# Attention with spatial reduction, then a gated feed-forward: query groups 8 to 11 turned by DMA, and the chunks lent to VectorE placed anew

## The chip, the cores and the metric

The kernel runs on one core of one Trainium2 chip. The metric is the device time of one execution in microseconds (us). Three runs of the kernel before gave a median of 942.97 us (942.91 to 943.38). One more execution was recorded by the hardware profiler. The engines are called PE (TensorE), DVE (VectorE), ACT (ScalarE), POOL (GpSimd) and SP (SyncE, which here only issues DMAs).

## The reference, cut to what matters

```python
# q (4, 12288, 128); kv (4, 384, 32, 128); w_sr (128, 128); w_in (128, 2048); w_out (2048, 128), all float32
kv_pool = kv.reshape(B, H // 4, 4, W // 4, 4, C).mean(axis=(2, 4))   # 4x4 mean: 768 keys per batch
k = v = kv_pool.reshape(B, -1, C) @ w_sr
s = (q @ k.transpose(0, 2, 1)) / sqrt(C)
a = softmax(s)                                                       # over the 768 keys
x = (a @ v).reshape(B * 12288, C)                                    # 49152 rows of 128
h = x @ w_in
out = (h * sigmoid(1.702 * h)) @ w_out
```

So each query row is compared with 768 pooled keys of its batch, the weighted values become a row of x, and each row of x goes through a feed-forward layer with 2048 hidden values.

## The kernel before, in words

The 49152 rows are cut into 96 groups of 512 rows (`NG`, `G`), and four groups make a slice (`SG`, 24 slices, `NS`). The attention of a group has 6 chunks (`JC`) of 128 keys; its feed-forward part has 16 chunks (`FCH`) of 128 hidden values. A chunk is one tile of 128 x 512. It is *filled* by one matmul of 512 columns into PSUM (L402 for attention, L688 for the feed-forward part), and one ACT instruction, over one, two or three chunks, applies the exponential (L404) or the gated activation (L690) and writes bfloat16 into a frame of `ag`. Later it is *drained*: four matmuls of 129 columns per attention chunk against values and a column of ones (L416), one matmul of 512 columns per feed-forward chunk against `w_out` (L698). `ag` has room for 102 chunks, so the drains can lag far behind the fills.

The work goes in two rounds (`R`): attention of groups 0 to 47, their feed-forward part, then the same for groups 48 to 95. Within the first round the six chunks of groups 0 to 7 are not in order of groups, since the keys come in chunk by chunk; they are listed by hand at L743, all 48 ahead of group 8. The first two ACT instructions take one chunk, the next 77 two, the others three (L742).

Not all chunks go through ACT. Those in the list `rolling` (attention) and `lent` (feed-forward) are computed on DVE from a PSUM bank by a chain of elementwise operations, 8 per exponential (`early_exp`) and 15 per gated activation (`lent_gelu`), and kept in the small tile `aside` instead of `ag`. Groups 48 to 51 (`early`) are computed on DVE wholly. A group whose last chunk is lent can only be drained to its end when the chain on DVE is done.

All instruction streams are written out by one planner, the loop at L885, which keeps a clock of its own with fixed costs (`COST`, `COPY`, `FIXED`, `CHUNK`), fills two steps ahead, and puts drains, transposes, pooling and DVE chains between the fills. The order on each engine is therefore fixed when the program is built; on the chip an engine runs its own stream in order and waits where a semaphore is not yet set. The tables `first`, `TURN`, `SUM`, `CAST` and `CAST_MOE` say by hand at which fill or at which group something is issued. A `gate()` (L593) is a one-element memset on DVE followed by one on POOL that waits for it: it holds back what POOL issues next until DVE has come to that place of its stream.

The fill of a group needs its queries with the 128 features on the partitions, in the tile `qT` of its slice (four buffers). There are two ways to get there:

- `load_q` (L265, POOL's queue, casting on the way) puts rows of float32 `q` as bfloat16 into a part of the tile `x`; `transpose_q` (L272) then turns a group with four PE transposes into PSUM and one copy into `qT` (by DVE; by ACT for group 0). Groups 0 to 9 come so.
- `cast_q` (L246, POOL's queue) writes a slice of `q` as bfloat16 into the DRAM tensor `q_bf`; `load_qT` (L251) turns the slice by one DMA transpose on SP's queue into `qT`, behind a memset of one column by DVE. Slices 3 and up come so. Groups 10 and 11, the second half of slice 2, come by `cast_q(2, 2)` and `load_rest(2, 2)` (L257), issued when group 5 begins.

POOL's queue at the start holds, in this order: queries of groups 0 to 7 mixed with chunks 1 to 5 of the keys and values (1 MB of float32 each), the load of groups 8 and 9, the cast of the second half of slice 2, the casts of slices 3 and 4, and behind a gate the cast of slice 5. SP's queue holds the first chunk of the keys, `w_sr`, then the DMA transposes in the order of the slices. The PE transposes of groups 8 and 9 are handed to the planner at fills 23 and 25 (`later`).

Of the kernel before, what the change touches and what calls it, by code (L numbers as in the profile page):

```python
# [26 lines left out]
def kernel(  # L27
# [8 lines left out]
    JC = J // 128  # L36
    d_ff = moe_w_in.shape[1]
    FCH = d_ff // 128
# [77 lines left out]
    def x_tile(s):  # L116
        return x[:, s % XS * SG:(s % XS + 1) * SG]
# [20 lines left out]
    def load_chunk(b, jc):  # L138

        a, ch = divmod(jc, HC)  # L140
        if b and jc in wide:
            nc.gpsimd.dma_start(out=wide[jc], in_=kv_r[b, a, ch])
            return
        t = x_tile(spots[jc] if b else XS - 1 - jc)
        nc.gpsimd.dma_start(out=t, in_=kv_r[b, a, ch])
        kv_tiles[b, jc] = t.rearrange("p (wp w1 c) -> p w1 wp c", w1=r, c=C)
# [12 lines left out]
    def add_row(jc):  # L159

        last, wp = False, None
        t = wide[jc].rearrange("p (wp e) -> p wp e", wp=r)
        narrow_sum = wide[jc].bitcast(BF).rearrange("p (wp e) -> p wp e", wp=r)[:, :, 4 * C:5 * C]
        for m in (0, 2):
            nc.vector.tensor_tensor(t[:, m:m + 2, 0:2 * C], t[:, m:m + 2, 0:2 * C], t[:, m:m + 2, 2 * C:4 * C], ADD)
            yield 3.2
        nc.vector.tensor_tensor(narrow_sum, t[:, :, 0:C], t[:, :, C:2 * C], ADD)
        added[jc] = narrow_sum
        extras.extend([(pool_added, 1, jc), (key_and_value, 1, jc)])
        last = True  # L170
        yield 3.3
# [34 lines left out]
    def add_kv(b, n):  # L206
        i, w = divmod(n, r)
        if n == 0:
            kv_sums[b] = kvs[0:Hp]
        for i2 in range(2):  # L210
            nc.gpsimd.dma_start(out=kv_sums[b][:, i2], in_=kv_p[b, i, w, :, i2],  # L211
                                **({"accum_op": ADD} if n else {}))
# [33 lines left out]
    def cast_q(s, lo=0):  # L246
        sl = slice(s * SG + lo * G, (s + 1) * SG)
        nc.gpsimd.dma_start(out=q_bf[sl, :].rearrange("(p i) c -> p (i c)", p=128),
                            in_=q_flat[sl, :].rearrange("(p i) c -> p (i c)", p=128))

    def load_qT(s):  # L251
        qTs[s] = qpool.tile([128, 1, SG], BF, name="qT")
        nc.vector.memset(qTs[s][:, 0, 0:1], 0.0)
        nc.sync.dma_start_transpose(out=qTs[s], in_=q_bf[s * SG:(s + 1) * SG, :])


    def load_rest(s, lo):  # L257
        qTs[s] = qpool.tile([128, 1, SG], BF, name="qT")
        nc.vector.memset(qTs[s][:, 0, lo * G:lo * G + 1], 0.0)
        nc.sync.dma_start_transpose(out=qTs[s][:, :, lo * G:], in_=q_bf[s * SG + lo * G:(s + 1) * SG, :])  # L260

    QS = 3
    qs = [x_tile(XS - 1 - JC - s) for s in range(QS)]

    def load_q(s, lo, hi):  # L265
        nc.gpsimd.dma_start(  # L266
            out=qs[s].rearrange("p (g e) -> p g e", g=4)[:, lo:hi, :],
            in_=q_flat[s * SG + lo * G:s * SG + hi * G, :].rearrange("(g p i) c -> p g (i c)", p=128, i=4))
# [30 lines left out]
    load_chunk(0, 3)  # L299
    load_chunk(0, 4)  # L300
    load_chunk(0, 5)
    load_q(2, 0, 2)
    cast_q(2, 2)
    cast_q(3)
    cast_q(4)

    ones = cpool.tile([128, 32], BF)
    nc.vector.memset(ones, 1.0)
# [70 lines left out]
        return K * len(free_frames())  # L379

    early = range(NG // R, NG // R + EARLY)
    rolling = [(i, JC - 1) for i in (28, 44, 45, 58, 59, 71, 73, 75, 95)]
    lent = [(g, FCH - 1) for g in (3, 7, 11, 13, 17, 19, 52, 53, 55, 56, 58, 60, 62, 65, 67, 69, 71, 72, 75, 77, 79, 81, 83, 84, 86, 88, 91, 93)]
    turn = [("a",) + c for c in rolling if c[0] < early[0]] + [("m",) + c for c in lent if c[0] < early[0]]
    turn += [("a",) + c for c in rolling if c[0] > early[-1]] + [("m",) + c for c in lent if c[0] > early[-1]]
    aside = agpool.tile([128, K, 512], BF, name="aside")
# [96 lines left out]
    def new_raw():  # L483
        nonlocal raw
        raw = qpool.tile([128, 1, SG], BF, name="qT")[:, 0, 0:2 * G].bitcast(F32)
# [75 lines left out]
    def early_fits(p, i, jc):  # L561
        if (i, jc) in rolling:
            group = seq[p][1][0][0] if seq[p][0] == "a" else seq[p][1][0][0] // (NG // R) * (NG // R) + NG // R - 1
            return (i // GB, jc) in vs and (i in turned or i // 4 in qTs and (i // 4 - 1 <= group // 4 if i >= 4 * QS else i - 2 <= group)) and len(used) > turn.index(("a", i, jc)) - K
        if (i, jc) in lent:
# [9 lines left out]
    def put_away(n, m):  # L575
        size = PART // 2 if n == 0 and m > FIRST + 1 else PART
        for o in range(m * PART, m * PART + PART, size):
            lo = n * XS * SG + o * T
            nc.sync.dma_start(out=x_bf[lo:lo + size * T, :].rearrange("(k p) c -> p k c", p=T),
                              in_=x[:, o * T:(o + size) * T].rearrange("p (k c) -> p k c", k=size))  # L580

    def bring_back(n, m):
        o = m * PART
        lo = n * XS * SG + o * T
        nc.sync.dma_start_transpose(out=x[:, o * T:(o + PART) * T].unsqueeze(1), in_=x_bf[lo:lo + PART * T, :])
# [7 lines left out]
    def gate():  # L593

        one = gate_tile[:, gates[0] % 8:gates[0] % 8 + 1]
        gates[0] += 1
        nc.vector.memset(one, 0.0)  # L597
        nc.gpsimd.memset(one, 0.0)  # L598

    TURN = {8: 3, 9: 4, 10: 5, 20: 6, 21: 7, 22: 8, 25: 9, 32: 10, 35: 11, 42: 12}  # L600
    SUM = {14: (0,), 15: (1,), 16: (2,), 17: (3,), 20: (4,), 21: (5,)}
    CAST = {0: [5], 13: [6], 14: [7], 15: [8], 16: [9], 26: [10, 11], 27: [12]}
    CAST_MOE = {20: 13, 21: 14, 22: 15, 23: 16, 33: 17, 34: 18, 35: 19, 36: 20, 37: 21, 38: 22, 39: 23}

    def background(i):

        first_round = i < GB * 2
        s = TURN.get(i, NS) if first_round else i // 4 + 3 if i % 4 == 0 else NS
        if s < NS:
            load_qT(s)  # L610
        if i == 5:
            load_rest(2, 2)
        if i in CAST:
            gate()
            for s in CAST[i]:
                cast_q(s)
        if i in (10, 12):
            gate()
            for jc in range(i % 10 * 3 // 2, i % 10 * 3 // 2 + 3):
                load_chunk(1, jc)  # L620
        for jc in SUM.get(i, ()):
            if jc in wide:
                sums.append(add_row(jc))
            else:
                extras.extend([(pool_chunk, 1, jc), (key_and_value, 1, jc)])
        if i in (28, 33, 38):
            put_away(0, (i - 28) // 5)
        if i in (31, 36, 41):
            bring_back(0, (i - 31) // 5)
        if i == 40:  # L630
            new_raw()
        if 4 * XS - LEAD <= i < 4 * XS:
            gate()
            add_kv(2, i - 4 * XS + LEAD)
        if i == 28:
            gate()
            nc.gpsimd.dma_start(out=w_in_sb, in_=moe_w_in)
        if i == 29:
            gate()
            nc.gpsimd.dma_start(out=w_out_sb, in_=moe_w_out.rearrange("(o p) c -> p o c", p=128))  # L640

    def background_moe(g):
# [16 lines left out]
        if g == 43:  # L659
            raw = None  # L660
            background(early[0])
# [19 lines left out]
    extras = []  # L681
# [102 lines left out]

    begun = set()

    def later(g):
        extras.append((transpose_q, g))

    def jobs(p):  # L790

# [9 lines left out]
    def prepare(p):  # L801
# [24 lines left out]
        16: [(key_and_value, 0, 4)],  # L826
        17: [(pool_chunk, 0, 5)],
        20: [(key_and_value, 0, 5)],
        23: [(later, 8)],
        25: [(later, 9)]}  # L830

# [51 lines left out]
    for n in range(len(seq)):  # L885
        fill(n + 2)
        jobs(n + 3)
        while True:
# [34 lines left out]
            kind, i, c = source[0]  # L923
# [58 lines left out]
```

## Time and profile before

| | |
|---|---|
| median of 3 runs | 942.97 us (942.91 to 943.38) |
| the profiled execution | 943.09 us |
| its span | 941.3 us |
| matmuls and PE transposes | 6218 |
| matmuls of 512 columns, L688 and L402 on ACT's side | 1508 and 543 |
| PE transposes of queries, L280 | 40 (ten groups) |
| activations, L690 and L404 | 506 and 208 |
| chunks on DVE from the lists: `lent`, `rolling` | 28, 9 |
| DMA transposes of queries, L254 and L260 | 21 and 1 |
| mean granted PE clock | 1.00 |

The span is what the profiler recorded from the first to the last instruction; the execution's own time is 1.8 us longer. In rows of the timeline the first number is the start in us from the span's start, the second the length; behind engine, line and operation stand the tiles written and read, and x how many instructions were merged. A matmul's length includes its way through the pipeline, so the distance between starts tells more than the length. In rows on DMAs the last number is the median time from issue to landing in us. POOL's and SP's issue rows (POOL L248, SPq L254) are the issue alone; the transfer goes on behind them.

### The profile page before, as it was taken

Reading aid. Unit: us, or ns where it says so; the run is one execution under the profiler, and the core shown is the slowest. Engines: PE = TensorE matmul, PEld = TensorE weight load, DVE = VectorE, ACT = ScalarE, POOL = GpSimd, SP = SyncE. Lnnn points to the kernel's source line nnn. Section 1 sums busy time; section 2 is a strip of 40 time slices with the busy share of each in tenths; the row PEclk is TensorE's granted clock in tenths of the full one; section 3 lists DMA queues with packets and bytes.
Section 4 is the critical chain, followed back from the end, with each engine's and each line's share of the span. In section 5 each row is a group of like instructions: output and inputs, shape, how many; then the busy total and the mean of one; then the engine's idle time right before and its main releaser. Section 6 shows DMA issues by size and latency. Waiting matters only on the chain.

```text
span 941.3 us, 15464 instructions
## 1 busy us (share of the span) xinstructions
PE 935.8 (99%) x6218; PEld 499.4 (53%) x6218; DVE 616.4 (65%) x1236; ACT 928.9 (99%) x722; POOL 75.2 (8%) x127
## 2 busy tenths in 40 slices
PE   9999999999999999999999999999999999999998
PEld 5777775444444444454447777744444444444444
DVE  6776376437477777777235755478787778778761
ACT  6999999999999999999999999999999999999998
POOL 3401014200003320000000000000000000000000
PEclk9999999999999999999999999999999999999999
DMA  9998969937679992774324956371222222222122
GB/s 211 223 285 180 197 140 136 136 73 157 145 145 173 165 129 39 120 124 94 62 57 104 172 130 135 70 133 34 42 38 35 44 34 45 34 40 41 33 46 45
DMA packets 379463, 99.91 MB, mean 106 GB/s; under 512 B 353536, under 2 KB 376960, under 8 KB 378272
## 3 DMA queue, kind: packets, MB, share of 16 engines
q1 hardware_dynamic: 350784, 64.06, 36.0%
q0 software_dynamic: 28336, 34.74, 22.1%
q8 instruction: 48, 0.79, 0.3%
q14 instruction: 23, 0.19, 0.1%
q10 hardware_dynamic: 272, 0.13, 0.0%
HBM read 52.49 MB, written 49.81 MB: 109 GB/s over the span
## 4 chain that ended last, share of the span: by engine, by line
PE 92%; ACT 6%; DMA 1%; POOL 0%; issue 0%; DVE 0%; POOLq 0%
PE banks L698 35%; PE banks L688 35%; PE banks L416 11%; PE banks L402 10%; ACT ag L404 6%; DMA x<-in_kv_dram 1%; PE banks L479 1%; PE banks L473 1%; PE banks L726 0%; PE banks L280 0%; PE banks L154 0%; POOL x L266 0%; PE banks L339 0%; PE banks L239 0%; DVE o_sb L734 0%
## 5 line engine op out<-in xcount | busy, mean ns | idle before, releaser
L690 ACT ACTIVATE ag<-banks 128x1536 bf16<-128x1536 f32 (+1 forms) x506 | 676.0, 1497 | 0.0
L688 PE MATMUL banks<-x,w_both 128*128 128x512 bf16 x1508 | 408.0, 379 | 0.0
L698 PE MATMUL banks<-ag,w_both 128*128 128x512 bf16 x1492 | 405.9, 379 | 0.0
L404 ACT ACTIVATE ag<-banks 128x1536 bf16<-128x1536 f32 (+2 forms) x208 | 246.0, 1365 | 3.4 <-PE banks L402 3.2
L698 PEld LDWEIGHTS <-w_both 128*128 128x128 bf16 x1520 | 148.6, 98 | 178.7 <-issue 1.1
L688 PEld LDWEIGHTS <-w_both 128*128 128x128 bf16 x1508 | 146.6, 98 | 172.2 <-issue 0.4
L416 PEld LDWEIGHTS <-ag 128*128 128x128 bf16 x2268 | 147.4, 98 | 49.6
L416 PE MATMUL banks<-v,ag 128*128 128x129 bf16 x2268 | 166.8, 220 | 0.0
L709 DVE STREAM_TRANSPOSE o_sb<-banks 128x512 f32<-128x512 f32 x95 | 67.9, 715 | 134.8 <-PE banks L698 132.6
L402 PE MATMUL banks<-qT,kT 128*128 128x512 bf16 x543 | 151.0, 379 | 0.3 <-DVE kT L187 0.2
L444 DVE RECIPROCAL rec<-banks 128x3 f32<-128x3 f32 x118 | 21.1, 179 | 83.5 <-PE banks L416 83.4
L447 DVE TENSOR_TENSOR x<-banks,rec 128x384 bf16<-128x384 f32 x118 | 65.8, 558 | 4.1
L402 PEld LDWEIGHTS <-kT 128*128 128x128 bf16 x543 | 45.2, 98 | 19.1 <-issue 0.7
L211 POOL DMA_DIRECT2D kvs<-in_kv_dram x32 | 40.3, 1278 | 54.8 <-DMA kvs<-in_kv_dram 54.2
L513 DVE SCALAR_TENSOR_TENSOR eb<-ea 128x512 f32<-128x512 f32 x61 | 42.1, 690 | 2.0
L509 DVE SCALAR_TENSOR_TENSOR eb<-ea 128x512 f32<-128x512 f32 x61 | 42.1, 690 | 1.8
L511 DVE SCALAR_TENSOR_TENSOR ee<-eb,ee 128x512 f32<-128x512 f32 x61 | 42.0, 688 | 1.7
L711 POOL DMA_DIRECT2D out_dram<-o_sb x2 | 1.3, 672 | 514.0 <-DVE o_sb L709 514.0
L519 DVE TENSOR_SCALAR ea<-banks 128x512 f32<-128x512 f32 x33 | 22.8, 692 | 27.0 <-PE banks L479 26.7
L530 DVE TENSOR_SCALAR qT<-banks 128x512 f32<-128x512 f32 x28 | 19.4, 692 | 30.1 <-PE banks L473 29.5
L598 POOL MEMSET gate_tile<- 1x1 f32 x38 | 8.8, 231 | 263.2 <-DVE gate_tile L597 263.2
L502 DVE TENSOR_SCALAR ea<-ea 128x512 int32<-128x512 f32 x61 | 26.7, 438 | 2.0
(96 smaller groups left out, 415.8 us busy)
## 6 DMA issues: line engine op xcount, KB each, us to landing
out_dram<-o_sb SPq DMA_DIRECT2D x378, 64.0 KB, 1.9
kvs<-in_kv_dram POOLq DMA_DIRECT2D x32, 384.0 KB, 6.5
q_bf<-in_q_dram POOLq DMA_DIRECT2D x21, 512.0 KB, 8.1
x_bf<-x SPq DMA_DIRECT2D x13, 768.0 KB, 5.6
x<-in_kv_dram POOLq DMA_DIRECT2D x6, 512.0 KB, 13.9
x<-in_kv_dram POOLq DMA_DIRECT2D x3, 1024.0 KB, 10.7
x_bf<-x SPq DMA_DIRECT2D x6, 384.0 KB, 4.7
x<-in_kv_dram SPq DMA_DIRECT2D x1, 1024.0 KB, 5.1
```

The lines of the kernel that those rows point to most:

```text
L211: nc.gpsimd.dma_start(out=kv_sums[b][:, i2], in_=kv_p[b, i, w, :, i2], **({"accum_op": ADD} if n else {}))
L402: nc.tensor.matmul(ps[:, k, :], kTs[i // GB][:, jc * 128:(jc + 1) * 128], rhs, start=True, stop=True)
L404: nc.scalar.activation(place([("a",) + c for c in chunks]), ps, AF.Exp, scale=scale)
L416: nc.tensor.matmul(av_of[u][:, k * (C + 1):(k + 1) * (C + 1)], weights(("a", i, jc))[:, o:o + T], vs[i // GB][:, jc, 0:C + 1], start=(jc = ...
L447: (nc.gpsimd if split else nc.vector).tensor_tensor(to, ps[:, :, 0:C], rec.unsqueeze(2).broadcast_to([128, TS, C]), MUL)
L509: nc.vector.scalar_tensor_tensor(b, a, P2[0], a, ADD, MUL)
L511: nc.vector.scalar_tensor_tensor(e, b, P2[1], e, ADD, MUL)
L513: nc.vector.scalar_tensor_tensor(b, a, P2[2], a, ADD, MUL)
L688: nc.tensor.matmul(ps[:, k, :], w_in_sb[:, fc * 128:(fc + 1) * 128], x[:, g % (4 * XS) * G:(g % (4 * XS) + 1) * G], start=True, stop=True)
L690: nc.scalar.activation(place([("m",) + c for c in chunks]), ps, AF.Gelu_apprx_sigmoid)
L698: nc.tensor.matmul(o_of[g], w_out_sb[:, fc, :], weights(("m", g, fc)), start=(fc == 0), stop=(fc == FCH - 1))
L709: nc.vector.transpose(o_sb, o_of.pop(g))
```

## The change

Groups 8 and 9 no longer come through `x` and PE. The whole slice 2 is cast to `q_bf` by one `cast_q(2)`, in the place of POOL's queue where the load of groups 8 and 9 and the half cast stood, and `load_qT(2)` is issued when group 0 begins, as the third instruction of SP's queue, where it waits for that cast. The casts of slices 3, 4 and 5 leave the start of POOL's queue: each is issued behind a gate of its own, handed to the planner at fills 18, 21 and 24. One of three places in `x` that held queries is no longer used so (`QS`). The lists change: `rolling` has 12 chunks instead of 9, `lent` 26 instead of 28, mostly at other groups.

```diff
-    QS = 3
+    QS = 2
     qs = [x_tile(XS - 1 - JC - s) for s in range(QS)]
...
     load_chunk(0, 5)
-    load_q(2, 0, 2)
-    cast_q(2, 2)
-    cast_q(3)
-    cast_q(4)
+    cast_q(2)
...
-    rolling = [(i, JC - 1) for i in (28, 44, 45, 58, 59, 71, 73, 75, 95)]
-    lent = [(g, FCH - 1) for g in (3, 7, 11, 13, 17, 19, 52, 53, 55, 56, 58, 60, 62, 65, 67, 69, 71, 72, 75, 77, 79, 81, 83, 84, 86, 88, 91, 93)]
+    rolling = [(i, JC - 1) for i in (32, 40, 47, 56, 57, 67, 68, 71, 78, 86, 89, 91)]
+    lent = [(g, FCH - 1) for g in (3, 6, 7, 11, 13, 17, 53, 54, 57, 59, 60, 65, 67, 69, 71, 72, 75, 77, 79, 81, 83, 85, 86, 89, 91, 93)]
...
-    CAST = {0: [5], 13: [6], 14: [7], 15: [8], 16: [9], 26: [10, 11], 27: [12]}
+    CAST = {13: [6], 14: [7], 15: [8], 16: [9], 26: [10, 11], 27: [12]}
...
-        if i == 5:
-            load_rest(2, 2)
+        if i == 0:
+            load_qT(2)
...
-    def later(g):
-        extras.append((transpose_q, g))
+    def cast_later(s):
+        gate()
+        cast_q(s)
...
         20: [(key_and_value, 0, 5)],
-        23: [(later, 8)],
-        25: [(later, 9)]}
+        18: [(cast_later, 3)],
+        21: [(cast_later, 4)],
+
+        24: [(cast_later, 5)]}
```

The lines from L306 to L786 stand 3 lines earlier in the changed kernel: L402 is L399 there, L416 is L413, L698 is L695.

## The prediction

> **What bounds the kernel now.** I read the page's head first, then the chain, then who waited for whom on ACT and PE.
>
> ```profile
> span 941.3 us, 15464 instructions
> PE 935.8 (99%) x6218; PEld 499.4 (53%) x6218; DVE 616.4 (65%) x1236; ACT 928.9 (99%) x722; POOL 75.2 (8%) x127
> PE 92%; ACT 6%; DMA 1%; POOL 0%; issue 0%; DVE 0%; POOLq 0%
> ```
> ```profile
> ACT x L329 <- DMA x<-in_kv_dram: 3.8, 1, 3.8
> ACT ag L404 <- PE banks L402: 3.2, 3, 2.3
> ```
>
> PE and ACT are both busy for 99%, and all of ACT's larger waits lie before 13.5 us. A busy PE could hide gaps, so I looked at starts in the timeline (start, length, engine, line, operands, count).
>
> ```profile
> 914.83 0.81 PE L688 MATMUL banks<-x,w_both 128*128 128x512 bf16 x3
> 915.48 0.81 PE L698 MATMUL banks<-ag,w_both 128*128 128x512 bf16 x3
> 916.13 0.81 PE L688 MATMUL banks<-x,w_both 128*128 128x512 bf16 x3
> ```
>
> Three matmuls start every 0.65 us, 0.216 each, without a hole. Counting the built program's PE stream with 0.216 per 512-wide matmul and 0.057 per 129-wide one gives some 922 us behind 12.8 us, where the trace needs 925: PE loses about 3 us to everything behind the start. So a shorter program must be shorter on PE and on ACT, and any wait of PE is added in full. DVE (65%) does not bound.
>
> **The start, where the change sits.** All 48 chunks of groups 0 to 7 go first, in 2 activations of one chunk and 23 of two; group 8's first pair is the next.
>
> ```profile
> 25.73 35.08 ACT L404 ACTIVATE ag<-banks 128x1024 bf16<-128x1024 f32 x38
> 30.93 0.39 PE L280 MATMUL banks<-ident,x 128*128 128x128 bf16 x4
> 31.16 0.39 PE L416 MATMUL banks<-v,ag 128*128 128x129 bf16 x4
> 32.83 0.39 PE L280 MATMUL banks<-ident,x 128*128 128x128 bf16 x4
> 33.05 0.39 PE L416 MATMUL banks<-v,ag 128*128 128x129 bf16 x4
> 33.28 0.59 PE L402 MATMUL banks<-qT,kT 128*128 128x512 bf16 x2
> ```
>
> The pair at 33.28 is group 8's: counting pairs in the PE stream gives its place, and ACT, at 0.92 per pair, takes it near 33.9. The two L280 rows are the transposes of groups 8 and 9. In the changed kernel this pair needs the whole DMA transpose of slice 2 (groups 8 to 11); its place in the stream stays, within 0.01 us of PE work.
>
> **The change, part by part.**
> (a) Eight PE transposes go: 31.16 - 30.93 and 33.05 - 32.83, 0.23 and 0.22, together -0.45 us on a saturated PE. Their two DVE copies (0.69 each, hidden) go too.
> (b) Chunks: 3 more exponentials and 2 fewer gelus run on DVE, so ACT has one chunk less: the built program has one 512-wide activation fewer, and as many 1536- and 1024-wide ones in sum.
>
> ```profile
> L690 ACT ACTIVATE ag<-banks 128x1536 bf16<-128x1536 f32 (+1 forms) x506 | 676.0, 1497 | 0.0
> ```
> 676.0/506 is 1.34 per three chunks; less the 0.92 of a pair, a chunk is 0.42, with its fixed part about 0.49. ACT so shrinks as PE does, and the sum takes -0.46 for (a) and (b) together. Bounds: 0 if PE's tail takes it back, -0.5. DVE loses 2 chains of 15 and gains 3 of 8 operations, at most 0.7 each: less work on an engine with 35% free. The placing itself costs nothing while chains end before their drains; if one is late, PE waits. The trace has no such wait, so its price is bounded by one operation's 0.7 below and a chain's remaining 8 x 0.7 = 5.6 above; I take 0.
> (c) The load of groups 8 and 9 (256 KB in bfloat16) and the half cast of slice 2 become one cast of slice 2 in the same place of POOL's queue. Here are their issues in that order, and what the landing view answers for these issues:
>
> ```profile
> 10.00 0.70 POOL L266 DMA_DIRECT2D x<-in_q_dram  x1 [1.92 <-DMA x<-in_kv_dram]
> 11.27 0.51 POOL L248 DMA_DIRECT2D q_bf<-in_q_dram  x1 [0.57 <-DMA x<-in_q_dram]
> 16.29 0.49 POOL L248 DMA_DIRECT2D q_bf<-in_q_dram  x1 [0.69 <-DMA x<-in_q_dram]
> ```
> ```profile
> q_bf<-in_q_dram POOLq DMA_DIRECT2D x1, 256.0 KB, 15.3
> ...
> q_bf<-in_q_dram POOLq DMA_DIRECT2D x1, 512.0 KB, 17.8
> ```
> The half cast lands at 11.27 + 15.3 = 26.6, the last of the three casts behind it at 34.1. As the new cast reads what both old transfers read, I take its landing at 26.5 (26.0 to 27.0).
> (d) SP then issues the transpose of 2048 rows. What this costs alone, and what beside casts, three rows show: the old half transpose, slice 3, and slice 6.
>
> ```profile
> 26.66 1.24 SPq L260 DMA_TRANSPOSE qT<-q_bf  x1
> 34.46 1.83 SPq L254 DMA_TRANSPOSE qT<-q_bf  x1
> 67.49 2.85 SPq L254 DMA_TRANSPOSE qT<-q_bf  x1
> 56.16 0.49 POOL L248 DMA_DIRECT2D q_bf<-in_q_dram  x1
> ```
> ```profile
> qT<-q_bf SPq DMA_TRANSPOSE x1, 8.4
> qT<-q_bf SPq DMA_TRANSPOSE x1, 4.2
> qT<-q_bf SPq DMA_TRANSPOSE x1, 5.4
> q_bf<-in_q_dram POOLq DMA_DIRECT2D x1, 512.0 KB, 14.1
> ```
> Alone: 34.46 + 4.2. Half the rows beside three casts: 8.4, landing at 35.1, that is 1.0 behind the last cast (34.1). Slice 6 beside the end of a cast: 67.49 + 5.4 = 72.9, 2.6 behind that cast (56.16 + 14.1 = 70.3). So a transpose that shares the engines with casts has landed 1.0 to 2.6 behind the last of them.
> (e) Casts 3, 4 and 5 were queued by 16.3 us; now each waits for a small DVE memset. By the new DVE stream these stand behind chunk 5's copy, behind one and behind five of the L428 sums that follow its keys and values:
>
> ```profile
> 26.01 0.29 DVE L157 CAST pTc<-banks 128x128 bf16<-128x128 f32 x1 [0.24 <-PE banks L154]
> 28.69 0.28 DVE L202 CAST v<-banks 128x128 bf16<-128x128 f32 x1
> 28.89 2.26 DVE L428 TENSOR_TENSOR ag<-banks,ag 128x387 f32<-128x387 f32 x4
> 419.26 0.09 POOL L598 MEMSET gate_tile<- 1x1 f32 x1 [7.38 <-DVE gate_tile L597]
> 419.49 0.49 POOL L248 DMA_DIRECT2D q_bf<-in_q_dram  x1
> ```
> ```profile
> q_bf<-in_q_dram POOLq DMA_DIRECT2D x1, 512.0 KB, 5.2
> ```
> From gate to cast is 0.3, so they are issued near 26.6, 29.8 and 32.0, and a cast with no queue ahead lands 5.2 later: 31.8, 35.0, 37.2. On POOL nothing behind them is due before 35.2 (the first L447). Slices 3 to 5 are turned from 34.5 on and needed from 45 on: hidden by 6 us. The buffers and SP's waits of those later turns are the same as before.
>
> The cast of slice 3 thus starts within 0.2 us of the transpose of slice 2, and the next two follow at 3.2 and 2.2 us. Alone the transpose lands at 26.5 + 4.2 = 30.7, 2.6 before 33.28; that margin is what one cast costs. Beside cast 3 alone it would land at 31.8 + (1.0 to 2.6) = 32.8 to 34.4; beside casts 3 and 4 at 36.0 to 37.6; beside all three at 38.2 to 39.8. The old half transpose was held up by all that was queued when it was issued. Cast 4 starts while the new, twice as long one is still held by cast 3, so I take two casts, at the near end, 36.0: a wait of 36.0 - 33.3 = 2.7 us, before which PE cannot start and behind which all its drains stand.
>
> **Weighing a rule.** The rows show a transpose behind casts. The Trainium skill, "DMA: Bandwidth & Descriptors", section on queues, rings and completion order, says that each DMA engine takes turns between its queues by whole packets. The rows on packets bear on it (queue, packets, MB, share of 16 engines; a window with one cast, and one with one transpose):
>
> ```profile
> q0 software_dynamic: 32, 0.52, 44.6%
> ...
> q1 hardware_dynamic: 2080, 0.52, 81.7%
> ```
> A cast is 2 packets per engine, in a 6.6 us window 2.9 us of each engine; the transpose is 130 small ones, 2.6 us. If turns are taken, each cast that arrives before the transpose ends puts its whole 2.9 us in front: 27.8 + 2.6 + 3 x 2.9 = 39.1, all three casts, a wait of 5.8. By that rule the time is the second rival's. The slow 8.4 us transpose agrees with it, the 5.4 us one only in part.
>
> **The sum.** The profiled execution took 943.09, its span 941.3 and 1.8 around it; the median is 0.12 less. 943.09 - 0.46 + 2.7 = 945.3, against the median 945.2. I call a change under 0.2% (1.9 us, 941.1 to 944.9) no difference that can be told.
>
> **Rivals.**
> 1. Not slower: the casts share instead of blocking, and the transpose, held by cast 3 at most, lands at 30.7 to 34.4. The wait is 0 to 1.1, the time 942.97 - 0.46 + (0 to 1.1) = 942.5 to 943.6. For it: the 5.4 us row, only 1.2 over the one alone. Against: the 8.4 us row with half the rows. It decides if the landing is before 35.7. Chance 0.30.
> 2. All three casts in front: landing 38.2 to 39.8, wait 4.9 to 6.5, time 947.4 to 949.0. For it: the old transpose did end behind all of them. Against: cast 5 is issued only at 32.0. Chance 0.15.
> 3. The new places leave a DVE chain late, and PE waits up to 5.6: 942.5 to 948.1, most likely near 945. Against: DVE has less to do, and the trace shows no such wait now. Chance 0.07.
> 4. Faster by over 0.2%: the 3 us that PE loses behind the start come back through the new places, 942.97 - 0.46 - (1.5 to 3) = 939.5 to 941.0. For it only the count above. Chance 0.08.
>
> **How the numbers follow.** My forecast, casts 3 and 4 in front, has 0.40: 944.9 to 946.7. Slower by over 0.2% is that (0.40), rival 2 (0.15) and most of rival 3 (0.05): 0.60. Within 0.2%: 0.30 and the rest of rival 3, 0.32. Faster: 0.08. The range leaves out rival 4 and the far end of rival 2: 942.3 to 948.0.
>
> **What would show it.** Right: PE at group 8's first pair (L399 there) waits some 2.7 us for the transpose of slice 2, ACT shows one wait of about 2 us near 34, and the landing of that transpose takes 9 to 10 us. Cast 3 is issued near 26.6. Wrong: a landing before 33.3 and no wait; a new DVE wait in PE's list; or ACT idle elsewhere. From the wait on, both streams should run as before, shifted, with the last activations 0.5 us earlier against it.

## The result, and the profile after

The changed kernel takes 945.84 us (median of 7 runs, 945.45 to 947.18), the kernel before, run beside it, 943.11 us (7 runs, 942.91 to 943.38). The ratio is 1.0033, with a 95% interval of 1.0021 to 1.0044: slower by 2.7 us by the medians, where 2.2 had been predicted. Two of the seven runs, at 947.1 and 947.2 us, showed a granted clock of 0.998 against 0.999 to 1.000 in the others. The profiled execution took 946.05 us.

The head of the page after and its chain line:

```profile
span 944.3 us, 15325 instructions
PE 929.6 (98%) x6096; PEld 499.2 (53%) x6210; DVE 609.1 (65%) x1228; ACT 928.7 (98%) x721; POOL 74.5 (8%) x128
...
PE 54%; ACT 42%; DMA 3%; issue 1%; DVE 0%; POOL 0%; POOLq 0%
```

The span grew from 941.3 to 944.3. The weight loads (6210 for 6218) and the activations (721 for 722) show that the work did shrink; PE's own busy time can't be compared, since about a hundred of its records are missing here. The chain's DMA share went from 1% to 3%; why its ACT share went from 6% to 42% is left open. Who waited for whom on PE, and on ACT:

```profile
PE banks L399 <- DMA qT<-q_bf: 2.9, 1, 2.9
...
PE banks L476 <- DMA qT<-q_bf: 0.3, 1, 0.3
```
```profile
ACT ag L401 <- PE banks L399: 3.8, 3, 2.9
```

These two rows of PE are new; no other wait of PE's list has changed by more than 0.2 us. In the timeline (start, length, engine, line, operands, count, and the idle time before with what ended it):

```profile
26.44 0.51 POOL L248 DMA_DIRECT2D q_bf<-in_q_dram  x1
26.70 4.88 SPq L254 DMA_TRANSPOSE qT<-q_bf  x1
36.22 0.60 PE L399 MATMUL banks<-qT,kT 128*128 128x512 bf16 x2 [2.93 <-DMA qT<-q_bf]
113.60 0.39 PE L476 MATMUL banks<-qT,kT 128*128 128x512 bf16 x1 [0.29 <-DMA qT<-q_bf]
```

Group 8's first pair waits 2.93 us for the transpose of slice 2. At 113.6 the chunk of group 40, one of the new places in `rolling`, waits 0.29 for slice 10's. The landing view for the window in which cast 3 (the cast of slice 3) and that first transpose are issued (KB and us from issue to landing):

```profile
q_bf<-in_q_dram POOLq DMA_DIRECT2D x1, 512.0 KB, 5.2
qT<-q_bf SPq DMA_TRANSPOSE x1, 9.5
```

26.7 + 9.5 = 36.2. What held it up is in the packets that started in windows of 0.4 us (queue, packets, MB, share of 16 engines, by the whole length of the packets that start there): the windows from 32.4, 32.8 and 35.2 us.

```profile
q1 hardware_dynamic: 452, 0.12, 127.1%
...
q0 software_dynamic: 16, 0.52, 607.8%
q1 hardware_dynamic: 80, 0.02, 22.5%
...
q0 software_dynamic: 32, 0.52, 613.2%
q1 hardware_dynamic: 32, 0.00, 7.8%
```

The transpose has 2080 packets. By the trace's records 2048 of them have 256 bytes, which are its whole 0.52 MB, and 32 have 4 bytes. None moved before 30.4, while cast 3's 16 large ones, started from 27.6 to 28.8, were under way. From 30.4 to 33.2 all but 32 of them went. At 32.8 each of the 16 engines then took up cast 4's one large packet, and the last 32 packets, two per engine, came only at 35.2. These 32 are the ones of 4 bytes (0.00 MB in the last row). So two casts held it, cast 3 at its head and cast 4 at its tail, and at the tail all data had been sent by 33.2: only its small last packets were still missing.

The span grew by 3.0 us although 0.46 of work should be gone. So PE loses some 3.46 us more than before beside its work, and 2.93 + 0.29 of these are the two waits.

### The profile page after: what moved, and what is told of

The parts are those of the page before. It is cut to its first block, busy times and chain, and to the rows that moved or that the text cites. A ratio compares the mean times of both kernels' runs of the same rounds, so it can differ in the third digit from the quotient of the medians.

```text
span 944.3 us, 15325 instructions
## 1 busy us (share of the span) xinstructions
PE 929.6 (98%) x6096; PEld 499.2 (53%) x6210; DVE 609.1 (65%) x1228; ACT 928.7 (98%) x721; POOL 74.5 (8%) x128
## 3 DMA queue, kind: packets, MB, share of 16 engines
q1 hardware_dynamic: 351808, 64.32, 36.6%
## 4 chain that ended last, share of the span: by engine, by line
PE 54%; ACT 42%; DMA 3%; issue 1%; DVE 0%; POOL 0%; POOLq 0%
ACT ag L687 36%; PE banks L695 17%; PE banks L685 17%; PE banks L413 10%; PE banks L399 8%; ACT ag L401 6%; DMA qT<-q_bf 2%; DMA x<-in_kv_dram 1%; PE banks L470 0%; PE banks L723 0%; PE banks L154 0%; PE banks L280 0%; PE banks L476 0%; ACT L401 0%; POOL x L266 0%
## 5 line engine op out<-in xcount | busy, mean ns | idle before, releaser
L695 PE MATMUL banks<-ag,w_both 128*128 128x512 bf16 x1468 | 400.4, 379 | 1.2
L695 PEld LDWEIGHTS <-w_both 128*128 128x128 bf16 x1520 | 148.7, 98 | 178.9 <-issue 0.7
L413 PEld LDWEIGHTS <-ag 128*128 128x128 bf16 x2256 | 147.0, 98 | 49.2 <-issue 0.6
L413 PE MATMUL banks<-v,ag 128*128 128x129 bf16 x2256 | 166.6, 220 | 0.6
L399 PE MATMUL banks<-qT,kT 128*128 128x512 bf16 x492 | 144.9, 379 | 4.9 <-DMA qT<-q_bf 2.9
L444 DVE TENSOR_TENSOR x<-banks,rec 128x384 bf16<-128x384 f32 x118 | 65.8, 558 | 4.1
L399 PEld LDWEIGHTS <-kT 128*128 128x128 bf16 x540 | 45.2, 98 | 21.9 <-DMA qT<-q_bf 3.1
L516 DVE TENSOR_SCALAR ea<-banks 128x512 f32<-128x512 f32 x36 | 24.9, 692 | 32.9 <-PE banks L476 32.7
L527 DVE TENSOR_SCALAR qT<-banks 128x512 f32<-128x512 f32 x26 | 18.0, 692 | 29.8 <-PE banks L470 29.4
L502 DVE TENSOR_SCALAR ee<-ea 128x512 int32<-128x512 int32 x62 | 27.0, 436 | 2.1
```

Of the source, the lines that this page charges most:

```text
L399: nc.tensor.matmul(ps[:, k, :], kTs[i // GB][:, jc * 128:(jc + 1) * 128], rhs, start=True, stop=True)
L413: nc.tensor.matmul(av_of[u][:, k * (C + 1):(k + 1) * (C + 1)], weights(("a", i, jc))[:, o:o + T], vs[i // GB][:, jc, 0:C + 1], start=(jc = ...
L444: (nc.gpsimd if split else nc.vector).tensor_tensor(to, ps[:, :, 0:C], rec.unsqueeze(2).broadcast_to([128, TS, C]), MUL)
L695: nc.tensor.matmul(o_of[g], w_out_sb[:, fc, :], weights(("m", g, fc)), start=(fc == 0), stop=(fc == FCH - 1))
```

## The experiments

Times are medians; each ratio is to the kernel before on the same chip.

### Casts later or earlier: e1, e2, e5

The three are the changed kernel with its casts at other fills, first e1 (cast 4 later), then e2 (no cast beside slice 2's transpose), then e5 (casts close together):

```diff
         18: [(cast_later, 3)],
-        21: [(cast_later, 4)],
-        24: [(cast_later, 5)]}
+        24: [(cast_later, 4)],
+        26: [(cast_later, 5)]}
```
```diff
-        18: [(cast_later, 3)],
-        21: [(cast_later, 4)],
-        24: [(cast_later, 5)]}
+        22: [(cast_later, 3)],
+        24: [(cast_later, 4)],
+        26: [(cast_later, 5)]}
```
```diff
         18: [(cast_later, 3)],
-        21: [(cast_later, 4)],
-        24: [(cast_later, 5)]}
+        19: [(cast_later, 4)],
+        21: [(cast_later, 5)]}
```

> The changed kernel with the casts of slices 4 and 5 handed out at fills 24 and 26 instead of 21 and 24; the cast of slice 3 stays at fill 18. Theory (the last packets of a transpose land behind a cast that arrives while it runs): only cast 3 is in front of the transpose of slice 2, which lands near 34.0 instead of 36.2, 7.3 us after its issue instead of 9.5; PE waits 0.7 us at group 8's first pair instead of 2.9, and the time is 2.2 us below the changed kernel's, 943.6. Rival (the wait comes from the cast of slice 3 alone): the landing stays at 9.5, the wait at 2.9, the time at 945.8. Rival (the wait is no loss since ACT sets the pace, and the loss lies elsewhere): the wait shrinks, the time stays at 945.8.

> The changed kernel with the casts of slices 3, 4 and 5 handed out at fills 22, 24 and 26 instead of 18, 21 and 24, so that none is under way while the transpose of slice 2 runs. Theory: that transpose lands about 4.2 us after its issue at 26.7, at 30.9, PE does not wait at group 8's first pair (33.3), and the time is 945.8 - 2.9 = 942.9 or a little below, at best 942.6, the kernel before less the 0.46 of PE and ACT. Rival (a late cast of slice 3 makes the transpose of slice 3 late): a new wait at group 12's first pair near 45 us, time 944 to 948.

> The changed kernel with the casts of slices 4 and 5 handed out earlier, at fills 19 and 21 instead of 21 and 24, so that all three casts arrive before the transpose of slice 2 has ended. Theory (it ends behind every cast that arrives while it runs): landing at 37.5 to 39, wait 4.3 to 5.7 us, time 947.2 to 948.6. Rival (it loses one cast's turn in the middle and no more): landing 36.2, wait 2.9, time 945.8.

The "chunk loads of batch 1" below are the six loads of 1 MB on POOL's queue that bring the keys and values of the second batch.

e1: 996.72 us, 1.0572 [1.0558, 1.0586]. e2: 973.01, 1.0310 [1.0276, 1.0344]. e5: 964.94, 1.0239 [1.0207, 1.0271]. PE's largest waits in these three, one fence each:

```profile
PE banks L178 <- DVE kvs L167: 27.6, 1, 27.6
PE banks L399 <- DMA qT<-q_bf: 18.4, 3, 11.5
```
```profile
PE banks L399 <- DMA qT<-q_bf: 25.6, 2, 25.4
```
```profile
PE banks L399 <- DMA qT<-q_bf: 26.1, 1, 26.1
```

For slice 2 the reason held: with cast 4 later its transpose landed 7.2 us after the issue and group 8 waited 0.39 us; with no cast beside it, 4.0 us and no wait. For the time it failed badly. In e1 and e2 the casts were pushed back, the transposes of slices 4 and 5 fell beside casts and the chunk loads of batch 1, and landed 29 to 56 us after their issue. In e5 slice 2's transpose and casts 4 and 5 held each other up: landings of 33.2, 28.8 and 29.6 us after their issues. Theory and rival had given the transpose a landing between 36 and 39 us on the clock, not at 60. The packets that started in e2 between 57 and 58 us, with slice 5's transpose beside loads:

```profile
q0 software_dynamic: 56, 0.39, 93.9%
q1 hardware_dynamic: 56, 0.01, 6.3%
```

One transpose packet of 256 bytes goes for each packet of POOL's queue (48 of 8 KB and 8 of 4 bytes by the trace's records), one for one, and together they fill the engines (93.9% and 6.3%). With 130 packets per engine and 56/16 = 3.5 of them per engine and us, a whole transpose takes 37 us in such company, against 4.0 alone.

### The new places alone, and the old ones: e3, e4

e3 is the changed kernel with the lists of before; e4 is the kernel before with those of the changed one, the same edit the other way round.

```diff
-    rolling = [(i, JC - 1) for i in (32, 40, 47, 56, 57, 67, 68, 71, 78, 86, 89, 91)]
+    rolling = [(i, JC - 1) for i in (28, 44, 45, 58, 59, 71, 73, 75, 95)]
...
```

> The changed kernel with the lists rolling and lent of the kernel before. Theory: the wait of 2.9 us at group 8's first pair stays, the small wait of a rolling chunk for a DMA transpose near 113.6 us (0.3 to 0.5 us) goes; ACT has one chunk more than the changed kernel, but PE the same work. Time 945.2 to 945.8. Rival (the new lists cost much of the loss): time 944.5 or below.

> The kernel before with the lists rolling and lent of the changed kernel, and nothing else changed: groups 8 and 9 are turned by PE. Theory (the DMA wait is the whole loss): no wait for a DMA transpose at group 8, time 942.6 to 943.6. Rival (the lists fit only the order they were made for, as the old lists in the changed kernel suggest, where the time rose by 6.6 us): 945 to 950.

e3: 952.41 us, 1.0093 [1.0078, 1.0108]. e4: 944.40 us, 1.0017 [1.0008, 1.0026]. PE's list in e3:

```profile
PE banks L399 <- DMA qT<-q_bf: 2.7, 1, 2.7
PE banks L685 <- ACT ag L687: 2.7, 5, 0.5
...
PE banks L399 <- DVE kT L201: 0.8, 1, 0.8
```

The wait at group 8 is there with the old places too, so the places don't cause it. But either set costs time in the other's order: the old ones in the changed kernel 6.6 us more than the new ones (952.41 against 945.84), the new ones in the kernel before 1.4 us (944.40 against 943.01), without a wait for a DMA transpose. Neither time lies in a range that was expected. The span of e4 is 942.6 for 941.3, with the same matmuls. Of e3's 6.6 us some 1.7 are the clock, by an estimate: it was granted at half for about 3.4 us behind the wait (see e11). In e3 PE has no drains left near 672 us and waits for ACT five times.

### The size of the casts' pieces: e7

```diff
-        nc.gpsimd.dma_start(out=q_bf[sl, :].rearrange("(p i) c -> p (i c)", p=128),
+        nc.gpsimd.dma_start(out=q_bf[sl, :].rearrange("(a p i) c -> p a (i c)", a=2, p=64),
...
```

> The changed kernel with every cast of q cut into 128 pieces of 8 KB of float32 instead of large contiguous pieces; the same bytes at the same places of POOL's queue. Theory (engines alternate between a transpose and another transfer by pieces, so the smaller piece costs a transpose packet less): the transpose of slice 2 lands 6 to 9 us after its issue instead of 9.5, and the wait at group 8's first pair is 0 to 2.5 us; time 943 to 945.5. Rival (only the bytes of the casts in front count): landing 9.5, time 945.8. Rival (more pieces, more turns lost): landing over 10, time above 947.

946.56 us, 1.0036 [1.0024, 1.0048]; the transpose took 9.2 us, the wait was 2.8. The theory fell: smaller pieces do not help. Each cast now is 128 packets where it was 16 large ones. The windows of 0.4 us from 32.8, 33.2 and 35.2:

```profile
q0 software_dynamic: 16, 0.07, 80.5%
q1 hardware_dynamic: 298, 0.08, 83.8%
...
q0 software_dynamic: 18, 0.07, 91.1%
...
q0 software_dynamic: 39, 0.10, 125.9%
q1 hardware_dynamic: 30, 0.00, 9.1%
```

The last 32 packets of the transpose, again those of 4 bytes, came near 35.2 once more, behind cast 4's pieces (118 of 128 had started by then), though between these pieces, over 7 on each engine, there were turns to take. So it is not one long packet that blocks them; they come behind the cast as a whole.

### Chunk 5 behind the cast of slice 2: e6, and its repair: e9

Both are the changed kernel; e9 has the second edit beside the first, with three loads at each of its two groups.

```diff
-    load_chunk(0, 5)
     cast_q(2)
+    load_chunk(0, 5)
...
-        17: [(pool_chunk, 0, 5)],
+        19: [(pool_chunk, 0, 5), (cast_later, 3)],
...
-        18: [(cast_later, 3)],
```
```diff
-    SUM = {14: (0,), 15: (1,), 16: (2,), 17: (3,), 20: (4,), 21: (5,)}
+    SUM = {15: (0,), 16: (1,), 17: (2,), 18: (3,), 20: (4,), 21: (5,)}
...
-        if i in (10, 12):
+        if i in (11, 12):
```

> The changed kernel with the cast of slice 2 ahead of chunk 5 of the keys in POOL's queue, chunk 5 pooled at fill 19 instead of 17, and the cast of slice 3 also at fill 19; casts of slices 4 and 5 at fills 21 and 24 as before. The transpose of slice 2 can start near 24.3 us and has chunk 5's load beside it instead of two casts. Theory (the loss is the wait of group 8's first pair for this transpose, and everything behind it is as in the changed kernel): it lands by 31, PE does not wait at 33.3, the time is 945.8 - 2.9 = 942.9 (942.5 to 943.5, up to 1 us more if chunk 5 comes late). Rival (the loss lies in the new lists or behind 50 us): the wait goes, the time stays above 945.

> The version in which the cast of slice 2 goes ahead of chunk 5 (the wait at group 8 is gone), and beside it the chunk loads of batch 1 are issued at groups 11 and 12 instead of 10 and 12, and the sums that use them one group later each. Theory (what was lost there, 6.9 us at 73.6, came from slice 5's transpose falling beside these loads): the loads start some 2.5 us later, behind the transposes of slices 4 and 5, these land 4 to 8 us after their issue, PE has no DMA wait over 1 us, and the time is 942.5 to 944. Rival: the loads still meet slice 5's transpose, which takes over 20 us, or the sums wait for the loads, and the time is over 946.

e6: 952.21 us, 1.0100 [1.0087, 1.0114]. e9: 954.64 us, 1.0144 [1.0108, 1.0179]. Slice 2's transpose landed after 4.6 us in both, and group 8 did not wait. The times missed all the same: both lie where the rivals put them. In e6 slice 5's transpose landed after 30.9 us beside the chunk loads, and PE waited 6.9 us for it. e9 missed its aim: the loads were issued at 42.23 us, not later than in e6 (42.07), because what came ahead of them on POOL were the divisions of group 8 on (L444) and not the gate. Slice 5's transpose landed after 43.9 us in its profile, with a wait of 19.3; that profile is of its longest run, 12 us above the median.

### Slice 2 turned in two halves: e8

```diff
-            load_qT(2)
+            load_first(2, 2)
+            load_second(2, 2)
```

The two new functions are `load_qT` for the rows of groups 8 and 9, and `load_rest` without a tile of its own. The order on PE, ACT and POOL stays.

> The changed kernel with slice 2 turned by two DMA transposes of 1024 rows, one behind the other, in place of one of 2048; casts, lists and the order on PE, ACT and POOL stay, DVE has one small memset more. Group 8's first pair then needs the first half only, group 10 the second. Theory (the loss is the wait of group 8 for the last packets of a long transpose that cast 4 holds up): the first half, held by cast 3 until about 28.8 us, lands by 33.3 at the latest, since its bulk is half of what went between 30.4 and 33.2; the wait of 2.9 us at group 8 falls to 0 to 0.5 us, the second half lands near 36 and delays nobody, and the time is 945.84 less 2.4 to 2.9, that is 942.9 to 943.5, level with the kernel before. Rival A (the landing of any transpose beside casts is bound to the last of them): the first half lands near 35 as well, and the time stays within 1 us of 945.8. Rival B (the loss is in the new places of the chunks and not in the wait): the wait goes, and the time stays above 944.7.

Six runs lay between 944.99 and 964.24 us (median 961.02, 1.0185 [1.0155, 1.0215]); the profile is that of 944.99. PE's list in it:

```profile
PE banks L408 <- DMA qT<-q_bf: 2.2, 1, 2.2
```

The first half, issued at 27.14, landed after 8.5 us at 35.6, near rival A's 35. Its 1024 data packets had gone by 32.8, its last 32, of 4 bytes, came at 34.4 and later, behind cast 4. The profile is of the shortest run; the median lies above all that was expected. In this profile the wait is 0.73 shorter than in the changed kernel's and the time 1.06 shorter (944.99 against 946.05). What makes the other runs 8 to 19 us longer was not seen, as they left no trace.

### The moved casts alone: e10

The kernel before, with this edit and without its cast of slice 5 at group 0:

```diff
     cast_q(2, 2)
-    cast_q(3)
-    cast_q(4)
...
+        18: [(cast_later, 3)],
+        21: [(cast_later, 4)],
+        24: [(cast_later, 5)],
```

> The kernel before with one part of the change: the casts of slices 3, 4 and 5 leave the start of POOL's queue and are issued behind gates at fills 18, 21 and 24. Groups 8 and 9 still come through PE, the second half of slice 2 by its half cast and half transpose, the lists are the old ones. Theory (the later casts cost nothing by themselves, the loss of the changed kernel is that group 8 waits for a transpose): no DMA wait on PE, since groups 10 and 11 are needed only near 39 us, and 943.1, between 942.6 and 944.0. Rival (the later casts push the transposes of slices 3 to 5 against the chunk loads, as in the versions without a wait at group 8): a DMA wait of several us between 40 and 100 us, and over 947.

966.06 us, 1.0207 [1.0148, 1.0266]. The theory fell: this part alone, with no transpose that group 8 needs, costs more than the whole change. PE's two waits, from the timeline, and the first chunk load:

```profile
59.39 0.22 PE L199 MATMUL banks<-pTc,w_sr_sb 128*128 128x128 bf16 x1 [4.16 <-DVE pTc L180]
88.93 1.03 PE L400 MATMUL banks<-qT,kT 128*128 128x512 bf16 x2 [16.51 <-DMA qT<-q_bf]
41.50 0.60 POOL L142 DMA_DIRECT2D kvs<-in_kv_dram  x1
```

Beside cast 5, issued at 32.84, slice 3's transpose takes 7.3 us in place of 4.2; those of slices 4 and 5 follow on SP's queue, and slice 5's is issued not at 39.85, as before, but about 41.7 (its landing at 88.9 less 47.2), when the loads have begun. It took 47.2 us to land (before: 4.1), and its packets went one for one with those of POOL's queue again, here between 60 and 61 us:

```profile
q0 software_dynamic: 51, 0.43, 128.1%
q1 hardware_dynamic: 51, 0.01, 6.2%
```

In the changed kernel the same late casts do no such harm: slice 5's transpose is issued at 43.28 and lands after 4.1 us, as POOL, behind the wait at group 8, issues the first load only at 44.91. The rows of slice 5's transpose and of the first load, from the kernel before and then from the changed kernel:

```profile
39.85 1.24 SPq L254 DMA_TRANSPOSE qT<-q_bf  x1
41.49 0.60 POOL L142 DMA_DIRECT2D kvs<-in_kv_dram  x1
```
```profile
43.28 1.24 SPq L254 DMA_TRANSPOSE qT<-q_bf  x1
44.91 0.59 POOL L142 DMA_DIRECT2D kvs<-in_kv_dram  x1
```

Both times the transpose has a lead of 1.6 us; in e10 it comes 0.2 behind the load. So the wait that costs 2.9 us also keeps these two apart.

### The casts early, as before: e11

The changed kernel, with cast 5 behind the gate at group 0 again:

```diff
     cast_q(2)
+    cast_q(3)
+    cast_q(4)
...
-        18: [(cast_later, 3)],
-        21: [(cast_later, 4)],
...
-        24: [(cast_later, 5)]}
+        }
```

> The changed kernel with the casts of slices 3 and 4 queued at the start behind that of slice 2, and that of slice 5 behind a gate at group 0, as before the change; the rest stays. By the prediction's rule (a transpose that shares the engines with casts lands 1.0 to 2.6 behind the last of them, which was 34.1 for the same transfers): landing 35 to 37, a wait of 2 to 3.5 us at group 8, 945 to 947, like the changed kernel. Rival (from the run with casts at fills 18, 19 and 21: whole transposes and close casts hold each other up): landing over 45, a wait over 10 us, over 955.

947.66 us, 1.0048 [1.0033, 1.0063]. The transpose of slice 2 landed at 36.5, 9.6 us after its issue, as the prediction's rule gives it (2.2 us behind the last cast, at 34.2): with all casts queued long before, nothing runs away as in e5. The time lies 0.7 above the expected range. The wait is only 0.1 us longer than in the changed kernel, and yet the span is 2.6 us longer. The row behind the wait in e11's timeline, and then the windows row of 38 to 40 us (busy time and count of PE, PEld, DVE, ACT and POOL, then the granted clock), first in e11, then in the changed kernel:

```profile
36.52 1.04 PE L401 MATMUL banks<-qT,kT 128*128 128x512 bf16 x2 [3.03 <-DMA qT<-q_bf]
```
```profile
38.00:40.00 2.00, 2.00 (x15) 1.45 (x14) 1.21 (x5) 1.30 (x2) 1.34 (x2) 0.50 0.00 0
```
```profile
38.00:40.00 2.00, 1.95 (x25) 1.51 (x24) 1.90 (x7) 1.99 (x3) 2.00 (x3) 1.00 1.03 233
```

In e11 PE had half its clock from about 35.6 us, in the wait, to 42.5 (0.88 over 42 to 44), 15 matmuls in 2 us for 25; in the changed kernel's profile it kept its full clock. The length of the wait does not decide this: in e7 and in e3, with shorter waits of 2.75 and 2.68 us, the clock fell too, from 36.6 to 40.0. The two rows of e7:

```profile
36.10 0.60 PE L399 MATMUL banks<-qT,kT 128*128 128x512 bf16 x2 [2.75 <-DMA qT<-q_bf]
38.00:40.00 2.00, 1.89 (x12) 1.38 (x12) 1.05 (x4) 1.02 (x1) 1.46 (x3) 0.50 1.17 265
```

So part of the difference between these versions is the clock, and where they all wait some 3 us at group 8, a difference of 1 or 2 us between them says little about the edit.

### Both casts at fill 21, loads later: e12

The changed kernel, with the sums of the first four chunks at groups 15 to 18 as in e9:

```diff
-        18: [(cast_later, 3)],
-        21: [(cast_later, 4)],
+        21: [(cast_later, 3), (cast_later, 4)],
...
-        if i in (10, 12):
+        if i in (12, 13):
```

> The changed kernel with the casts of slices 3 and 4 both at fill 21 and that of slice 5 at 24, and the chunk loads of batch 1 at groups 12 and 13 (issued near 43.5 us) in place of 10 and 12, the sums of the first four chunks one group later. Theory: cast 3 moves data only from 30.8 us on, when the transpose of slice 2 (issued 26.7, 4.0 us alone) has ended, so no wait at group 8; the transposes of slices 3 to 5 end before the loads begin to move data near 44.7, and the time is 942.5 to 944. Rival: slice 4's or slice 5's transpose still runs beside casts or loads and takes over 10 us, and the time is over 946.

944.90 us (10 runs, 944.26 to 949.81), 1.0027 [1.0016, 1.0039]. PE's list:

```profile
PE banks L336 <- DVE col L308: 1.0, 1, 1.0
PE banks L154 <- DMA x<-in_kv_dram: 0.4, 1, 0.4
PE banks L399 <- DVE kT L201: 0.4, 1, 0.4
PE banks L199 <- DVE pTc L180: 0.4, 1, 0.4
```

The wait went as the theory had it: slice 2's transpose took 4.2 us, no wait for a DMA transpose is left, and slice 5's transpose, which still ran beside the loads (8.2 us from 43.32, the first load issued at 44.13), delays nobody. The time did not follow: 944.90 is above the 942.5 to 944 expected. The span of the profile falls from 944.3 to 942.6, not to the 941.4 that a wait of 2.93 would free: two new waits of 0.4 us for the later sums are in it. With the work of 0.46 less, this version's profile still ends 1.3 us behind that of the kernel before, so PE loses some 1.8 us more than there, and only about half of this is told by the two waits. No version beat that one.

## Why the prediction was right

The forecast was that cast 3 and cast 4 hold the transpose of slice 2 until 36.0 and PE waits 2.7 us.

- Step (a) and (b), -0.46 us: the weight loads fell by 8 and the activations by one. The two waits, 3.22, less this term make 2.8 of the span's 3.0. Not measured by itself.
- Step (c), landing of the cast of slice 2 at 26.5: it was issued in the same place and landed after 16.7 us, and the transpose was issued at 26.70.
- Step (e), casts at 26.6, 29.8 and 32.0: they came at 26.44, 29.59 and 32.08.
- Step (d), the landing: 36.2 for 36.0, the wait 2.93 for 2.7. That two casts count and not one or three is what the packets show. The exact reading differs: cast 3 held the whole transpose, cast 4 its last 32 packets, and cast 5 started as these left. That the size came out so well is in part luck, since two misses cancel: cast 4 took 6.4 us and landed at 36.0, not at 35.0 (29.8 + 5.2), and the transpose came 0.2 behind it, not 1.0. e2 and e12 show that without a cast beside it the transpose takes 4.0 to 4.2 us and the wait is gone; rival 1 (a landing by 34.4) and rival 2 (38.2 or later) are out.
- The new places at 0: e4 and e12 speak against it. They lose 1.3 us of span more in the order of before, a second wait of 0.29 us stands at 113.6, and without the wait at group 8 there are still about 1.8 us lost that were not lost before (0.8 of them from e12's own later sums); where the other 1.0 goes was not found. In the changed kernel little of it shows: 3.46 are lost, and 3.22 of them are the two waits.
- "Slices 3 to 5 are hidden by 6 us" was true and rested on something I had not named. e10, e6 and e9 show that the later casts push slice 5's transpose against the chunk loads; only the wait at group 8, with the loads 3.4 us later than in e10, kept them apart. Had the wait been absent with the casts where they are, e6 and e10 suggest a loss of 9 to 23 us, which no rival held.
- The price of 1.0 to 2.6 us behind the last cast held where the casts had been queued long before (2.2 in e11). In e5, where three casts met a whole transpose at its start, the transpose landed 0.2 behind the last of them (59.8 and 60.0); what failed there, by over 20 us, was the price of a cast, 28.8 and 29.6 us for the last two instead of 5.2.
- The rule of turns by whole packets, from the Trainium skill, "DMA: Bandwidth & Descriptors", section on queues, rings and completion order: by it all three casts stood in front, 39.1; measured was 36.2. The sum had all casts arrive before the transpose ends, but its data had gone by 33.2, before cast 5 moved any. The one-for-one rows of e2 and e10 agree with the rule. The last two packets per engine, of 4 bytes, are not explained by it: in e7, with casts in short pieces, they still waited for nearly the whole cast. What orders a transpose's last packets no run here shows.

## What to carry to other kernels

Before moving a DMA to a queue that looks free, list every transfer that can be under way with it and with what it pushes back: here a move that was to save 0.46 us of work cost a wait of 2.9 us, and the same late casts without that wait cost 9 (e6) to 23 us (e10). Keep whole DMA transposes away from casts and from large loads: whole ones took 7 to 33 us beside casts here and 29 to 56 beside loads, for 4.0 to 4.2 alone. And a wait that looks like pure loss may hold two transfers apart: take it away in an experiment before pricing it.

## What was not expected of the hardware

- A transpose beside loads: 4.0 to 4.2 us alone, 29 to 56 us beside 1 MB loads (e1, e2, e6, e9, e10), one 256-byte packet for each packet of the other queue, with the engines full in e2's row. Which comes first decides: issued 1.6 us ahead of the first load the transpose takes 4.1 us (the changed kernel: 43.28 and 44.91), 0.8 ahead of it 8.2 (e12), 0.1 to 0.5 behind it 31 to 47 (e2, e6, e9, e10).
- A transpose that has sent all its data has not landed: its 32 packets of 4 bytes came 2 us later, with the end of a cast (the changed kernel, e7, e8). With no cast beside it they followed the data at once (e2, 29.6 to 30.4).
- The granted clock can fall in a wait of some 3 us, and the wait's length does not tell whether: one of 2.93 us left it at 1.00, those of 2.68 (e3) and 2.75 us (e7) put it to 0.50 for 3.4 us, and one of 3.03 us (e11) for 6.8, which cost most of the 2.6 us between e11 and the changed kernel. The Trainium skill, "TensorE: Matmul & The Clock Gate", Part 1, has the clock halved after an idle window of about 3.4 us that runs freely. Where the wait lies in such a window would explain why its length does not decide, which is argued and not shown; that 2.68 us were enough is less than the section says.
- The same program with two half transposes ran anywhere from 945 to 964 us (e8), where the kernel before, run beside it, stays within 0.3 us.
